# Tables of order, PSUM banks and engines replaced in a fused attention and mixer kernel

## The chip, the cores and the metric

The kernel runs on one core of a Trainium2 chip. A core has five engines that each work through their own list of instructions in order: TensorE (PE, matmuls; its weight loads are shown as PEld), VectorE (DVE), ScalarE (ACT), GpSimd (POOL), and SyncE (SP), which here only issues DMAs. Engines wait for each other on semaphores. Matmuls write to PSUM, a memory of eight banks of 512 fp32 columns on 128 partitions; everything else lies in SBUF. The metric is the device time of one run in microseconds (us), the median of several runs.

## The reference

Eight batches, eight heads, 576 positions, head size 64:

```
scores = (q @ k.T) / 8, block-causal mask of 64 x 64 blocks
attn   = softmax(scores) ; x = attn @ v, heads side by side -> x[576, 512]
theta  = x @ w_theta ; zr = x * cos(theta) ; zi = x * sin(theta)
y      = w_tok_r @ zr + w_tok_i @ zi        (mixing over positions)
u      = x + y
out    = u + relu(u @ w_ch)
```

All inputs are wide; weights arrive as 64-bit floats. The kernel splits most operands into a high and a low fp16 part and adds three products (high x high, low x high, high x low). Queries and keys of batches 0 to 2 are multiplied as fp32.

## The kernel before

**Parts.** The work is cut into 3,404 parts, each a Python function that emits one or a few instructions of one engine. `add(...)` enters a part with its key, what it needs, the PSUM labels that it takes, and the engines that may do it ("A" ACT, "D" DVE, "P" POOL). 371 labels take a PSUM bank, and 915 parts can run on more than one engine. Nothing else in the code decides the order: `emit` (L236) walks the table `ORDER` (L37), in which each number is a part, takes each label's bank from the string `BANKS` and each part's engine from the string `PLACES`. As engines work in order, `ORDER` fixes every engine's list, the DMA queue on SP included.

**Attention.** A pair is two heads of one batch; there are 32 pairs and 64 heads n. For pair p the parts are `s1` (wide scores, both heads, into the two-bank tiles s0 and s1, L589 and mask L596), `s2` (narrow scores, into two other banks), `sd` (first-row scores, L617, into 64 columns of bank 7). For head n: `m` (maxima, DVE, L633), `mn` (bias, L641), `e` (exponentials, ACT, L646), `high` and `low` (fp16 parts of the probabilities p, L431, L433, L436), `turn` (DMA transposition of p, L665), `weighted` (the sum with v, L680, into the output columns of bank 7), `normalise` (three DVE steps, L692, L694, L698), `half` (a small DMA). Heads of the first half of pieces (n < 16) come in two pieces, A and B; later ones as one, "all". The wide tiles exist once, so `s1` of a pair waits until the exponentials of the pair before have read them.

**Mixer.** For batch b: `xh`, `xl`, `xt` (parts of x and their transposition), `theta` (L816, L819), `turns`, `rest`, `size` and `sines` (angles, L828, L834, L849, L851), `z` (product with x, L860), `zh` and `zl` (its parts, L436), `mix` (L884), `xs` (L889), `u` (L893), `uh` and `ul` (L900), `c` (channel product, L907), `relu` (L913 or L915), `out` (L923), `store`. Every `theta`, `mix` and `c` group takes one of banks 0 to 6 until it is read.

**Weights.** At the start 17 blocks of weights (`w`) are loaded, narrowed and split on ACT, DVE and POOL, and their largest values found with matmuls (`wa`, L494).

**PSUM tiles.** The eight banks are six tiles: two tiles of two banks and four of one bank each. The framework orders accesses to a tile; bank 7 holds both the output sums and the first-row scores:

```python
two_banks = [ps.tile([P, 1024], F32, name=f"s{n}") for n in range(2)]
banks = [two_banks[n // 2][:, 512 * (n % 2):512 * (n % 2) + 512] for n in range(4)]
banks += [ps.tile([P, 512], F32, name=f"g{n}") for n in range(4, 8)]
o = o_bank[:, 0:NI * (D + 1)].rearrange("p (a c) -> p a c", a=NI)
s_first = [o_bank[:, 384 + 64 * i:448 + 64 * i] for i in range(2)]
```

Of the kernel before, what the change touches and what calls it, by code (L numbers as in the profile page):

```python
# [37 lines left out]
    8, 9, 158, 160, 335, 10, 11, 0, 1, 16, 17, 2, 56, 340, 364, 363, 372, 373, 374, 336, 339, 57, 40, 3, 350, 58,  # L38
    18, 24, 351, 32, 352, 59, 19, 41, 386, 42, 390, 375, 334, 341, 25, 26, 362, 20, 414, 353, 354, 48, 33, 376, 104,
    49, 164, 43, 338, 361, 365, 366, 34, 337, 355, 105, 342, 345, 391, 401, 162, 343, 27, 415, 35, 106, 107, 367,  # L40
    344, 50, 51, 72, 368, 369, 346, 165, 4, 385, 347, 402, 108, 403, 412, 64, 163, 166, 413, 65, 167, 404, 416, 66,
    73, 387, 417, 418, 5, 168, 28, 12, 169, 389, 13, 80, 392, 170, 67, 81, 82, 171, 21, 388, 172, 423, 383, 60, 74,
    83, 393, 161, 96, 97, 394, 98, 29, 136, 137, 395, 138, 139, 396, 159, 437, 36, 332, 99, 88, 75, 89, 90, 52, 466,
    100, 436, 424, 425, 441, 348, 442, 465, 91, 405, 333, 112, 349, 120, 397, 398, 464, 463, 439, 37, 44, 356, 357,
    438, 140, 84, 68, 22, 113, 121, 45, 53, 384, 358, 359, 452, 377, 114, 173, 76, 178, 370, 426, 176, 453, 61, 454,
    440, 427, 69, 77, 474, 443, 85, 475, 444, 447, 467, 378, 92, 419, 406, 399, 420, 93, 115, 101, 30, 141, 445,
    371, 122, 123, 142, 446, 151, 143, 144, 379, 14, 421, 180, 380, 116, 31, 434, 435, 468, 54, 381, 469, 70, 94,
    86, 448, 476, 487, 449, 489, 515, 491, 407, 128, 488, 455, 456, 494, 490, 6, 470, 471, 514, 518, 129, 495, 130,
    492, 493, 503, 519, 520, 504, 400, 408, 409, 410, 15, 145, 428, 360, 422, 516, 429, 505, 539, 131, 496, 430,
# [12 lines left out]
    155, 648, 649, 641, 95, 670, 646, 604, 611, 650, 693, 645, 1856, 669, 1868, 651, 1864, 1854, 656, 1855, 564,
    612, 1857, 652, 613, 698, 614, 615, 657, 658, 653, 654, 691, 694, 692, 720, 1858, 697, 678, 659, 633, 695, 626,
    1865, 1862, 699, 1859, 197, 634, 679, 680, 1866, 1867, 635, 696, 1908, 1909, 1863, 1910, 636, 1911, 689, 1889,
    660, 700, 701, 1914, 1870, 707, 681, 1915, 708, 709, 1872, 744, 1893, 119, 690, 1899, 1900, 719, 1885, 682, 702,
    637, 1871, 674, 703, 718, 1901, 1881, 655, 1916, 1876, 721, 661, 1917, 662, 1912, 710, 2004, 200, 722, 675, 723,
    2007, 724, 199, 683, 1888, 729, 704, 1894, 711, 1873, 1880, 730, 663, 1907, 676, 1892, 201, 664, 1918, 749,
    1895, 1896, 1913, 665, 1897, 725, 2005, 1919, 684, 1902, 1903, 1877, 677, 1898, 2008, 685, 731, 686, 687, 743,
    1884, 742, 1878, 1879, 1904, 202, 747, 748, 712, 1874, 705, 732, 733, 203, 713, 726, 1875, 785, 204, 195, 706,
    746, 745, 750, 1882, 1883, 205, 1886, 1887, 766, 765, 753, 1944, 1945, 1890, 206, 764, 755, 754, 767, 768, 2006,  # L70
    1938, 1946, 1939, 1891, 666, 156, 1940, 1941, 714, 715, 207, 1942, 716, 751, 752, 734, 1947, 790, 208, 756, 757,
    191, 826, 727, 728, 1948, 135, 1937, 740, 735, 741, 736, 1949, 771, 737, 738, 781, 772, 688, 1943, 769, 2009,
    717, 770, 773, 2010, 1905, 783, 787, 786, 1920, 784, 788, 789, 2023, 2011, 2024, 758, 807, 791, 759, 792, 796,
# [1103 lines left out]
```

## Time and profile before

| | |
|---|---|
| median of 3 runs | 668.34 us (667.21 to 670.35) |
| profiled execution, span | 668.2 us |
| PE busy | 615.9 us, 92% |
| DVE busy | 570.6 us, 85% |
| ACT busy | 508.4 us, 76% |
| POOL busy | 393.8 us, 59% |
| mean granted clock of PE | 0.959 |

The profile gives no other time of the profiled execution than its span, from the first to the last instruction. Busy time is the union of an engine's instructions; those of the same engine can overlap a little. Tiles are called by their names: "s" is a two-bank PSUM tile, "g" a one-bank PSUM tile, "t" the exponentials, "p" their parts, "pt" the transposed p, "xT" the transposed x (later the result). A granted clock of 1.00 is 2.4 GHz and 0.50 is 1.2 GHz.

### The profile page before, as it was taken

To read this page: it belongs to the slowest core of one execution; us is meant where nothing else is said; L and a number is where in the kernel's file an instruction comes from. 1 tells how busy PE (TensorE), PEld (TensorE's weight loads), DVE (VectorE), ACT (ScalarE), POOL (GpSimd) and SP (SyncE) were. 2 spreads that over 40 slices of the span, in tenths; PEclk is the share of its full clock that TensorE was granted. 3 is DMA by queue.
4 is the path that set the end of the run, shared out by engine and by line. 5 is a ranking of instruction groups with operands and counts; after the bars stand their busy time and mean duration, and the time that the engine had idled before them with its cause. 6 is when DMAs were issued, how large, how long until landed. Compare 5 with 4: busy or idle time off the path is not lost. (4 is left out here: it accounts for less than half of the span.)

```text
span 668.2 us, 18051 instructions
## 1 busy us (share of the span) xinstructions
PE 615.9 (92%) x7372; PEld 459.6 (69%) x7374; DVE 570.6 (85%) x1136; ACT 508.4 (76%) x776; POOL 393.8 (59%) x411
## 2 busy tenths in 40 slices
PE   5477796999999999999999998999999998999997
PEld 3155554876788578776778766875786586857775
DVE  4987897998998998989989889999998998846474
ACT  5997878776997998978998899889997986325111
POOL 4355564876575446564675748664777476673340
PEclk9578896999999999999999999999999998999999
DMA  8999999998989596989869897889797655840002
GB/s 347 381 235 231 207 165 196 248 197 147 233 197 214 126 242 122 194 170 183 220 169 169 164 222 164 192 169 202 186 207 156 120 89 117 172 82 1 19 36 88
DMA packets 268514, 116.57 MB, mean 174 GB/s; under 512 B 256016, under 2 KB 256016, under 8 KB 268432
## 3 DMA queue, kind: packets, MB, share of 16 engines
q1 hardware_dynamic: 268432, 115.43, 78.5%
q8 instruction: 57, 0.93, 0.6%
q14 instruction: 25, 0.20, 0.1%
HBM read 42.01 MB, written 9.44 MB: 77 GB/s over the span
## 5 line engine op out<-in xcount | busy, mean ns | idle before, releaser
L884 PEld LDWEIGHTS <-zh 128*128 128x128 f16 x1152 | 112.7, 98 | 30.4 <-issue 1.6
L884 PE MATMUL g<-wT_h,zh 128*128 128x288 f16 x405 | 115.9, 286 | 0.3 <-DVE xT L923 0.3
L884 PE MATMUL g<-wT_l,zh 128*128 128x288 f16 x405 | 115.8, 286 | 0.0
L884 PE MATMUL g<-wT_h,zl 128*128 128x288 f16 x405 | 115.8, 286 | 0.0
L680 PE MATMUL g<-v,pt 128*128 128x65 f16 x2880 | 104.8, 197 | 10.5 <-DVE xn L698 4.4
L680 PEld LDWEIGHTS <-pt 128*128 128x128 f16 x2880 | 101.0, 100 | 17.7 <-issue 9.6
L633 DVE TENSOR_REDUCE m<-s 128x1 f32<-128x576 f32 (+3 forms) x134 | 86.4, 668 | 12.0 <-PE s L596 11.8
L436 POOL TENSOR_TENSOR p<-t,p 128x512 f16<-128x512 f32 (+4 forms) x31 | 69.8, 2254 | 43.7 <-ACT p L431 26.5
L431 ACT CAST p<-t 128x1600 f16<-128x1600 f32 (+4 forms) x62 | 79.7, 1289 | 7.8 <-DMA pt<-p 6.8
L436 DVE TENSOR_TENSOR p<-t,p 128x1600 f16<-128x1600 f32 (+4 forms) x49 | 80.4, 1643 | 4.3 <-ACT p L431 3.8
L860 POOL TENSOR_TENSOR aa<-aa,xn 128x256 f32<-128x256 f32 (+1 forms) x63 | 51.5, 829 | 28.1 <-ACT aa L849 25.5
L816 PEld LDWEIGHTS <-xT 128*128 128x128 f16 x384 | 36.6, 98 | 43.8 <-DMA xT<-xp 2.4
L884 PEld LDWEIGHTS <-zl 128*128 128x128 f16 x576 | 56.4, 98 | 14.4 <-POOL m L641 0.4
L646 ACT ACTIVATE t<-s,m,size 128x576 f32<-128x576 f32 (+1 forms) x80 | 59.2, 777 | 8.1 <-POOL m L641 6.0
L907 PEld LDWEIGHTS <-wch_h 128*128 128x128 f16 x512 | 48.1, 98 | 14.7 <-issue 2.9
L633 DVE TENSOR_REDUCE m<-g 128x1 f32<-128x320 f32 (+2 forms) x154 | 53.5, 369 | 2.3 <-PE g L596 0.7
L646 ACT ACTIVATE t<-g,m,size 128x192 f32<-128x192 f32 (+2 forms) x100 | 49.2, 533 | 5.4 <-POOL m L641 3.5
L436 POOL TENSOR_TENSOR zl<-aa,zh 128x512 f16<-128x512 f32 (+1 forms) x38 | 44.7, 1181 | 12.9 <-PE g L617 6.9
L907 PE MATMUL g<-ul,wch_h 128*128 128x288 f16 x164 | 46.9, 286 | 2.8 <-DVE ul L900 2.8
L884 PE MATMUL s<-wT_l,zh 128*128 128x288 f16 x171 | 48.9, 286 | 0.0
L884 PE MATMUL s<-wT_h,zl 128*128 128x288 f16 x171 | 48.9, 286 | 0.0
L884 PE MATMUL s<-wT_h,zh 128*128 128x288 f16 x171 | 48.9, 286 | 0.0
(187 smaller groups left out, 1632.8 us busy)
## 6 DMA issues: line engine op xcount, KB each, us to landing
rv<-in_v SPq DMA_DIRECT2D x16, 768.0 KB, 5.3
rq<-in_q SPq DMA_DIRECT2D x16, 640.0 KB, 5.3
rk<-in_k SPq DMA_DIRECT2D x16, 576.0 KB, 5.5
out<-xT SPq DMA_DIRECT2D x32, 288.0 KB, 2.5
w_raw<-in_w_tok SPq DMA_DIRECT2D x5, 576.0 KB, 5.4
pt<-in_w_tok SPq DMA_DIRECT2D x4, 576.0 KB, 7.4
w_raw<-in_w_theta SPq DMA_DIRECT2D x4, 512.0 KB, 7.0
w_raw<-in_w_ch SPq DMA_DIRECT2D x4, 512.0 KB, 5.6
```

What stands on the lines that cost most here:

```text
L431: nc.scalar.copy(out=out, in_=x)
L436: engine_of(on).tensor_tensor(out=out, in0=x, in1=y, op=ALU.subtract)
L633: nc.vector.tensor_reduce(out=self.m[:, i:i + 1], in_=self.scores_of(i), axis=AX.X, op=ALU.max)
L646: nc.scalar.activation(out=t_parts[self.hh][:, to:to + n], in_=self.scores_of(i), func=AF.Exp, scale=self.scales()[0], bias=self.m[:, NI + ...
L680: nc.tensor.matmul(o[:, i, :], lhsT=source[:, block, :], rhs=vv[:, slot, hh, :], start=first, stop=last)
L816: nc.tensor.matmul(g, lhsT=xT[:, xx + i, :], rhs=ww[:, dt, :], start=first, stop=last)
L860: engine_of(on).tensor_tensor(out=cd, in0=cd, in1=self.xns[dt][:, i0:i0 + ni, :], op=ALU.mult)
L884: nc.tensor.matmul(g, lhsT=zz[:, kk, cols], rhs=ww[:, kk, ts], start=(n == 0 and kk == k0 and nn == 0), stop=n == 4 and kk == k0 + ni - 1 ...
L907: nc.tensor.matmul(g[:, 0:HS], lhsT=ww[:, dt, e * P:(e + 1) * P], rhs=uu[:, dt, th * HS:(th + 1) * HS], start=dt == 0 and n == 0, stop=dt ...
```

## The change

The three tables are replaced; no other line of the kernel changes, and the parts are the same. The diff, cut to the first lines of each table:

```diff
 ORDER = [
-    8, 9, 158, 160, 335, 10, 11, 0, 1, 16, 17, 2, 56, 340, 364, 363, 372, 373, 374, 336, 339, 57, 40, 3, 350, 58,
...
 BANKS = (
-    "4556164551001236001234501234601235601235401231001236501236401235401234601235601235601235601234501235401235401235"
...
+    "4504666153001236401236501234601234601235601235401231001234501236401235401234601235601235601235601234501235401235"
...
 PLACES = (
-    "DAAPDAPAAADAAAAAAPDAPDAAPAAAAAPAAPAAPAAPAADAAPADAAAAPDPPPPDDDDAPPDAPPAPDDDDAPPDADPPPDAPPPPADADPAPPAPPPPAPADPPDDP"
...
+    "DAPDAADAADAAPAAAAADAADAPPAADAADAADAADAAAAAAAAPAAPDADPADDPPPDPDPDAPADPDDPADDAPDPADDADPPPDADAPADPADPDDPPPPPADDAPPA"
```

With the numbers turned back into parts, PE's list begins as follows (the head of each list, to the end of the first theta; `s1.0` is the wide scores of pair 0):

```
before: s2.0 sd.0 s2.1 s1.0 s1.1 sd.1 wa.0 vm.0 wa.1-3 s2.2 s1.2 weighted.0.A wa.4 weighted.0.B sd.2 wa.5-10
        weighted.1.B wa.11 wa.12 weighted.1.A s1.3 sd.3 weighted.2.B s2.3 weighted.2.A weighted.3.A weighted.3.B s2.4
        weighted.4.A weighted.4.B s1.4 sd.4 weighted.5.A weighted.5.B sd.5 weighted.6.B wa.13-16 ...
after:  s2.0 sd.0 s1.0 sd.1 s2.1 wa.0 wa.1 s1.1 wa.2 wa.3 vm.0 wa.4 s2.2 s1.2 sd.2 wa.5 weighted.0.B weighted.0.A
        sd.3 wa.6-10 weighted.1.B wa.11 weighted.1.A wa.12 s1.3 s2.3 weighted.2.A weighted.2.B weighted.3.A sd.4
        weighted.3.B s2.4 sd.5 weighted.4.A weighted.4.B s1.4 weighted.5.A weighted.5.B wa.13-16 vm.1 weighted.6.B ...
```

71 of 371 bank entries and 327 of 915 engine entries differ. Engine entries before and after: POOL 367 and 331, ACT 295 and 296, DVE 253 and 288. By kind, on DVE before and after: `low` 49 and 58, `z` 61 and 73, `zl` 19 and 24, the third step of the weights 4 and 10, `qh` and `kh` 0 and 7, `v1` 2 and 4, `xh` 2 and 7, `relu` 28 and 24, `mn` 27 and 23, `size` 15 and 11, `xs` 15 and 13.

## Rows read from the trace of the kernel before

**Rows 1.** The page: busy us, share of span, instructions of each engine.

```profile
PE 615.9 (92%) x7372; PEld 459.6 (69%) x7374; DVE 570.6 (85%) x1136; ACT 508.4 (76%) x776; POOL 393.8 (59%) x411
```

**Rows 2.** Stretches: length, busy us by engine (instructions), clock, DMA share, GB/s.

```profile
0.00:20.00 20.00, 8.98 (x48) 6.18 (x48) 10.11 (x21) 10.56 (x18) 7.46 (x32) 0.99 0.92 353
20.00:40.30 20.30, 12.44 (x54) 7.00 (x57) 18.61 (x40) 19.69 (x36) 10.53 (x11) 0.50 0.98 322
40.30:84.60 44.30, 32.98 (x464) 26.12 (x463) 36.83 (x94) 36.57 (x65) 25.78 (x28) 0.81 1.12 223
84.60:134.00 49.40, 43.21 (x466) 30.29 (x465) 45.00 (x83) 39.46 (x63) 31.25 (x33) 0.86 0.98 205
134.00:550.00 416.00, 406.92 (x5267) 304.43 (x5264) 384.95 (x770) 363.04 (x537) 263.64 (x259) 1.00 0.85 178
550.00:668.20 118.20, 111.34 (x1093) 85.53 (x1089) 75.06 (x134) 39.09 (x63) 55.17 (x51) 0.99 0.33 75
```

**Rows 3.** PE in order of time, start: start us, length, instruction, [wait <-releaser].

```profile
10.45 2.19 PE L589 MATMUL g<-rk,rq 64*128 64x320 f32 x12
...
23.76 4.11 PE L589 MATMUL s<-rk,rq 64*128 64x512 f32 x16 [7.17 <-ACT t L646]
...
47.25 0.98 PE L680 MATMUL g<-v,pt 128*128 128x65 f16 x15 [2.14 <-ACT t L646]
...
73.52 0.43 PE L617 MATMUL g<-rk,rq 128*128 128x64 f32 x2 [1.11 <-DVE xn L698]
...
106.59 4.11 PE L589 MATMUL s<-rk,rq 64*128 64x512 f32 x16 [3.43 <-DMA rk<-in_k]
...
113.06 0.69 PE L617 MATMUL g<-rk,rq 128*128 128x64 f32 x2 [2.25 <-DVE xn L698]
```

**Rows 4.** Waits of PE from 134 us on: us in total, times, longest.

```profile
PE g L907 <- DVE ul L900: 2.8, 2, 2.6
PE s L907 <- ACT t L646: 2.5, 2, 1.9
...
PE g L680 <- DVE xn L698: 1.2, 2, 0.8
...
PE g L680 <- DVE m L633: 0.4, 1, 0.4
PE s L589 <- DVE xT L923: 0.3, 1, 0.3
PE g L589 <- ACT t L646: 0.3, 1, 0.3
PE g L884 <- DVE xT L923: 0.3, 1, 0.3
```

**Rows 5.** Waits of ACT over the whole span, two of them.

```profile
ACT s L913 <- PE s L884: 1.7, 1, 1.7
...
ACT t L646 <- DVE xn L698: 0.6, 1, 0.6
```

**Rows 6.** Groups by shape: count, busy us, mean ns of one, idle before.

```profile
L900 DVE SCALAR_TENSOR_TENSOR ul<-u,u_scales,uh 128x576 f16<-128x576 f32 x32 | 29.8, 940 | 2.4 <-POOL uh L427 1.5 <-ACT uh L423 0.6
...
L436 DVE TENSOR_TENSOR p<-t,p 128x1536 f16<-128x1536 f32 x15 | 26.6, 1773 | 0.5 <-issue 0.3 <-ACT p L431 0.2
L860 DVE TENSOR_TENSOR rr<-rr,xn 128x256 f32<-128x256 f32 x28 | 14.8, 529 | 0.0
...
L436 DVE TENSOR_TENSOR zl<-rr,zh 128x512 f16<-128x512 f32 x9 | 7.4, 820 | 0.0
...
L436 DVE TENSOR_TENSOR p<-t,p 128x512 f16<-128x512 f32 x3 | 2.3, 769 | 0.0
```

**Rows 7.** In order of time, 550 to 555 us.

```profile
550.42 3.41 POOL L436 TENSOR_TENSOR p<-t,p 128x1600 f16<-128x1600 f32 x1
550.79 3.66 DVE L900 SCALAR_TENSOR_TENSOR ul<-u,u_scales,uh 128x576 f16<-128x576 f32 x1
...
554.50 0.28 PE L907 MATMUL g<-ul,wch_h 128*128 128x288 f16 x1 [2.58 <-DVE ul L900]
```

More of the change, by code (lines that the diff above doesn't have):

```diff
@@ L37 @@
 ORDER = [
[176 rows of a table removed]
[171 rows of a table added]
 ]
 BANKS = (
-    "4556164551001236001234501234601235601235401231001236501236401235401234601235601235601235601234501235401235401235"
-    "4012346012354012346012346012345012354012356012356012346012356012365012346012364012365012365246551650445606454041"
-    "6540151630666461566050425316646355451406665420444500465601466501605440544155446405425450164156455646416040451634"
-    "52245163452601620132435450513216524"
+    "4504666153001236401236501234601234601235401231001234501236401235401234601235601235601235601234501235401235401235"
@@ L220 @@
+    "4012346012354012346012346012345012354012356012356012346012356012365012346012364012365012365246511650445606454021"
+    "6540151344666061566050435256666455450616566350154500465601415661602510544155446450425420154166455546416040451626"
+    "34532653264501205145632130623406543"
 )
 PLACES = (
-    "DAAPDAPAAADAAAAAAPDAPDAAPAAAAAPAAPAAPAAPAADAAPADAAAAPDPPPPDDDDAPPDAPPAPDDDDAPPDADPPPDAPPPPADADPAPPAPPPPAPADPPDDP"
-    "DDPPPDAPPAPPADPPDDPADPAPPADPAPADADPADDADPAPAPADDADPPAPPPDPPADPADAPADPADAADPADDAPAAPPADPAPAAADADPADPPADADPADAPADA"
@@ L229 @@
-    "DAAADAPPAPPPAPDPAPPDAPPPPPPDPPPPAPPPPPPDPPDDAPDADAPDDADDAAAADAAPPDAPPDDDDADPDAPDPADDDAPDPPDDPADPPDDDDAPDPPPPPDPP"
-    "PADDADDPDPPDDADAAAA"
+    "DAPDAADAADAAPAAAAADAADAPPAADAADAADAADAAAAAAAAPAAPDADPADDPPPDPDPDAPADPDDPADDAPDPADDADPPPDADAPADPADPDDPPPPPADDAPPA"
+    "DPAPADAPPDPPADPPDDPADPADPADPADAPADPADPADPAPAPADPADAPAPPPDPPADPADAPADPDDDAADADDAPAAAPADPAPAAAPADPADDPDDADPADAPADA"
+    "DPADADAPDDPAPAAAPADPADPPPPADPAPDDPDAPDADAAAPPPDADAAPDADPADDPAPADPADAAADADPADAAAPADDPDDPPDADDAPAPAPADDADAAAPADPAP"
@@ new lines @@
+    "AAADDDPAPAAPDAPPDPPPPPADDADPPPPPDAPADAAAPPPDPDAPPPPDDDADPPAPDDAPPPAPDPAPPDAPPPPDPADDPDDDAADADADAADADAPDDDAAAADDP"
+    "PDDPPPPAPPPAPPDAPPDAPPDADDDAPPPPPDDPDPADADAPPDAADAAAAAPAPAPDDAAADDPPAPDPPDDPAPPDPDPPDPDDAPPDAPPPAPPDADDPAPPPPAPP"
+    "PDADAAAAAAAPPPDPDDADAADPPADPPAPDPAPDPPDDDAPPPAPDDAPPDPDDDAPPDAPPAPAPAPPDDAADDDDADAPAPADDAAAAPPAPPDPPPPPPPPPPDDAP"
+    "DDAPDDAPPDAPDPAPDPDPDADAPAPADDAADAADADDPAPAPAADAAPPPDPPPPDPPPDPADPPPDPDAPDDADPDAPDDAPPDDPDAPPPDDAAAAADDAADPADAPD"
+    "DAAADAPPPDPDAPPDPPDDPDPDAPDPAPPPADPPADDPAPPPAPDDPDDDPAADDAADAAADPPPPADDAAADPDADPDPPDDPPPDPPDPPPDPADDPPPPDDDPDADD"
@@ L231 @@
+    "PPPDPDPDAPADDAAAADA"
 )
```

5 lines of the change are left out of this document (removed), and 346 rows, old and new, of the table ORDER.

## The prediction, made before the result was known

> **What bounds the kernel now.** I read the busy shares first. TensorE (PE) is busy 615.9 of 668.2 us [rows 1], so the time is PE's work plus PE's idle time plus what the half-speed clock costs. The stretches say where the idle time lies. Subtracting PE busy from the length of each stretch [rows 2] gives 11.0, 7.9, 11.3 and 6.2 us of idle in the four stretches up to 134 us (36.4 us together), 9.1 us in the 416 us from 134 to 550, and 6.9 us after that. So PE is 98% busy from 134 us on, and 73% before. The granted clock is 0.50, 0.81 and 0.86 of full speed from 20 to 134 us: its lower level, 1.2 GHz, is granted in stretches where PE has been idle, and it is 1.00 where PE is always fed.
>
> The other engines show who makes PE wait. VectorE (DVE) is busy 385.0 of 416 us from 134 to 550 (92.5%), ScalarE (ACT) 87%, GpSimd (POOL) 63% [rows 2]. So in the long middle PE is the bound, and DVE is the next one, 31 us of idle away from it. Up to 134 us no engine is full: between 20 and 134 us DVE is busy 100.4 of 114 us and ACT 95.7, and PE stands still for chains that run through both. The largest single waits of PE there are 7.17 us for an exponential of ACT, 3.43 us for the load of k, 2.25 and 1.11 us of the first-row scores for the normalisation's read of the output bank, and 2.14 us of a weighted sum for an exponential [rows 3]. After 134 us the waits are a dozen small ones, 2.8 us for DVE's low part of u and 2.5 us for exponentials the largest [rows 4].
>
> **The change part by part.** *What stays.* The 3,404 parts and their arithmetic are the same, so PE has the same 7,372 matmuls. Only gaps, clock and waits can move. Laid side by side, the tables are near twins: adding up the matmul time of PE's new list, the PE work ahead of each pair's wide scores differs from the old by at most 2 us for the pairs I compared.
>
> *Order at the start.* The old list has PE run the narrow scores of pair 1 before the wide scores of pair 0; the new one has them after (s2.1 behind s1.0). Those 12 matmuls take 2.19 us and stand just ahead of the wide scores [rows 3]. The wide scores of pair 1 later wait 7.17 us for pair 0's last wide exponential. With pair 0's scores ready 2.2 us sooner, and ACT's new list with some 2.6 us less weight conversion ahead of that exponential (11.6 us instead of 14.2 by the shortest record of each kind), I take 2.2 us off this wait. It carries to the end only if what is late next moves too: DVE, with 5 to 6 us more ahead of the last maxima of pairs 2 and 3.
>
> *First-row scores and the output bank.* Bank 7 holds the output sums and the 64 columns of first-row scores. sd.4 stood behind its pair's wide scores and waited 1.11 us for the previous head's normalisation; now it lies between the two pieces of one head's sum, where no read stands before it, so 1.1 us go. weighted.1.B waited 2.14 us for the exponential of first-row scores of pair 2; pair 2's first-row scores are now issued ahead of weighted.0.B instead of behind weighted.0: about half of that wait goes, 1.1 us. sd.6, with 2.25 us, stays where it was [rows 3]. Of these 4.4 us (2.2, 1.1, 1.1) I count half, 2.2 us: DVE and ACT are at 88% and 84% there, so half of a freed gap fills with their next lateness. Bounds: 4.4 us gained, or nothing.
>
> *Waits inside a PSUM tile in the middle.* Banks 0 and 1 are one tile, 2 and 3 another. A rectification waited 1.7 us for a mixing matmul, which never writes its bank; and an exponential 0.6 us for a normalisation, though both only read [rows 5]. So accesses to one tile do wait on each other, and a list made without them has PE arrive too early. Of PE's waits after 134 us I put 5.0 us to that class: 2.5 us for exponentials (a channel product in a wide-score bank), 1.2 and 0.4 us of the weighted sum, 0.3 us three times for exponentials or bank releases [rows 4]. 71 of 371 bank entries change. Counting places in the lists where PE comes back to bank 7 after a read with under 1.5 us of PE work between, there are 12 before and 9 after; the two-bank tiles have 8 before and 6 after. That is a modest thinning (and weighted.50 now follows weighted.49 with nothing between): I take half, 2.5 us. Bounds: 5.0 us, or a loss of 2 us if new tight places weigh more.
>
> *Engines.* POOL loses 36 entries, DVE gains 35, ACT gains one. The three largest kinds on DVE: nine low parts p (at most six of 0.77 and three of 1.77 us, 9.9 us), twelve z products (0.53, 6.4 us) and five low parts of z (0.82, 4.1 us) [rows 6], 20.4 us. DVE casts of q and k are not in the trace; seven of them between 0.53 and 0.82 us [rows 6] are 4 to 6 us. The rest nearly cancels against fewer rectifications, biases and absolute values. I take 22 us on DVE: about 7 before 134 us, 13 from 134 to 550, the rest behind. What hides them is DVE's idle: 31 us of 416 shrink to 18, 95.7% busy. If that cover fails wholly, 13 us come out on PE; if DVE was never the late one, 0. The nearest row is the only big stall DVE made, 2.58 us [rows 7], and its cause is not DVE's load: I take 0.8 us.
>
> That row shows something else. The low part of u that PE waited for took 3.66 us on DVE, against 0.94 us on average [rows 6, 7]. It began 0.37 us into a POOL low part of 3.41 us and ended 0.62 us behind it. The Trainium skill, SBUF — State Buffer (Who interferes with whom), says that a DVE instruction with two SBUF inputs contends with a GpSimd one that reads SBUF, and that the later of the two blocks fully. By that rule this trace agrees, and each low part taken off POOL would free DVE as well as POOL. The sum would then have no charge for DVE, 663.5 us.
>
> **Sum.** The profiled execution took 668.2 us, 0.1 below the median of the three runs, 668.34. 668.2 - 2.2 - 2.5 + 0.8 = 664.3 us.
>
> **Rivals.** *A, the forecast:* 664.3, from 661 to 667. *B, the gains are displaced:* every gap removed turns into another, since lists of equal length with equal PE work ahead of each pair leave the same chains. For it: sd.6, the wait for k at 106.6 us and the chain through the sines stay where they were. Against it: the first order change is real. 668 us. *C, slower, DVE becomes the bound between 134 and 550 us:* DVE's work there rises to 398 us. If it must stand idle for as long as before, 31 us, the stretch takes 429 us, 13 us more: 681; if for 24.5 us, 422.5, 6.5 us more: 674.7 us, which I take. It decides from where DVE still needs more than 18 us of its idle. For it: 95.7% leaves little room, and a list in fixed order can't use a gap that comes at the wrong place. Against it: POOL's share falls with it, so that DVE's inputs come sooner. *D, POOL's unloading frees DVE, and all of the start's gaps close:* 4.4 us at the start, 5.0 us in the middle and 2.6 us of the stall at 554.5 [rows 7]; 668.2 - 12.0 = 656.2. Against it: the POOL low part that blocked DVE at 550.4 is still POOL's in the new table, and still next to that ul. *That the change does not count what it says* would look like B.
>
> **How the numbers follow.** A 0.50, B 0.22, C 0.16, D 0.12. A measurement of this kernel tells about 0.5% from no change, that is 665.0 and 671.7 us. Of A's range the part below 665.0 holds 0.62; with D and a little of B faster is 0.31 + 0.12 + 0.03 = 0.46. No change: 0.18 of A, 0.17 of B, 0.03 of C, 0.38. Slower: 0.16. The range reaches from D to most of C: 656.5 to 673.5 us. The likeliest case alone has 661 to 667.
>
> **What would show it.** The wait of the second wide scores under 5.5 us (7.17 before); sd.4 without a wait for the normalisation; PE idle before 134 us near 34 us; PE waits on exponentials and normalisation after 134 us near half of 5.0 us; DVE near 592 us busy, POOL near 355. Wrong: DVE over 96% between 134 and 550 with PE idle above 12 us there (C); the clock staying low longer at the start, or PE idle unchanged in both parts (B).

## The result: slower by 1%

| | before | after |
|---|---|---|
| median, 4 runs each | 668.19 us (667.21 to 670.35) | 674.45 us (673.61 to 675.86) |
| ratio | | 1.0098 (95%: 1.007 to 1.0125) |
| span of the profiled execution | 668.2 us | 674.0 us |

The changed kernel is 6.3 us slower. The time was forecast at 664.3 us, with a gain as the likeliest outcome; the direction was wrong. Wherever a run's time and span are both on record, the time is 1.7 to 2.2 us longer. So the profiled execution of the old kernel, with a span of 668.2 us, is most likely the slowest of its four, 670.35 us. In the profile after, a line of the kernel has a number smaller by 6 (by 5 in the kernels of the experiments).

The page's busy times, as in [rows 1]:

```profile
PE 614.9 (91%) x7374; PEld 452.8 (67%) x7374; DVE 589.5 (87%) x1171; ACT 507.1 (75%) x777; POOL 351.1 (52%) x375
```

VectorE has 18.9 us more, GpSimd 42.7 us less: 592 and 355 had been forecast. The stretches, with the columns of [rows 2]:

```profile
0.00:20.00 20.00, 9.10 (x52) 5.88 (x52) 11.06 (x25) 11.21 (x19) 6.48 (x33) 1.00 0.93 365
20.00:40.30 20.30, 11.99 (x56) 6.70 (x56) 19.67 (x41) 20.27 (x37) 5.92 (x7) 0.62 1.14 317
40.30:84.60 44.30, 33.23 (x473) 26.28 (x474) 38.97 (x94) 35.09 (x61) 19.76 (x25) 0.79 1.03 230
84.60:134.00 49.40, 42.22 (x482) 29.20 (x481) 45.78 (x97) 42.59 (x69) 29.44 (x36) 0.97 1.00 205
134.00:550.00 416.00, 398.79 (x5133) 293.21 (x5133) 388.06 (x765) 353.62 (x525) 226.28 (x222) 1.00 0.82 174
550.00:674.00 124.00, 119.57 (x1185) 91.49 (x1180) 85.92 (x153) 44.35 (x71) 63.24 (x57) 1.00 0.38 81
```

From 134 to 550 us TensorE stands idle for 17.2 us (416 less 398.79), where it was 9.1. VectorE is busy for 93.3% of it, hardly more than before; by this row alone it is not the bound. But the row cuts at the same times, not at the same work; the section on VectorE's load below has the cut at equal work. At the start TensorE, in order of time, answers to [rows 3]:

```profile
10.54 4.11 PE L583 MATMUL s<-rk,rq 64*128 64x512 f32 x16
...
20.80 3.59 PE L583 MATMUL s<-rk,rq 64*128 64x512 f32 x16 [4.00 <-ACT t L640]
...
29.89 0.26 PE L368 MATMUL g<-diag,ones 128*128 128x128 bf16 x1 [4.31 <-POOL diag L362]
...
56.44 0.77 PE L674 MATMUL g<-v,pt 128*128 128x65 f16 x11 [2.93 <-DVE xn L692]
...
107.59 0.43 PE L611 MATMUL g<-rk,rq 128*128 128x64 f32 x2 [2.54 <-DVE xn L692]
```

The first two rows are the wide scores of pairs 0 and 1: the second waits 4.00 us, not 7.17. New waits stand behind it (4.31, 2.93). TensorE's waits behind 134 us, as in [rows 4]:

```profile
PE g L674 <- DMA pt<-p: 2.8, 4, 1.2
PE g L674 <- DVE xn L692: 2.7, 4, 1.2
PE g L901 <- DVE u L887: 2.4, 1, 2.4
PE g L901 <- DVE ul L894: 1.6, 1, 1.6
PE s L901 <- ACT t L640: 1.3, 2, 0.9
PE s L810 <- ACT t L640: 1.3, 1, 1.3
PE g L583 <- DVE xT L917: 1.2, 2, 0.6
PE s L368 <- POOL diag L362: 1.0, 1, 1.0
```

Those on exponentials are hardly less (1.3 and 1.3; 2.5 and 0.3 before), and those on the normalisation `xn` have grown (2.7; 1.2 before), as have those on `xT` (1.4 in all; 0.8 before) and on the transposed probabilities `pt` (2.8; 1.1 before, not among the lines of [rows 4]). The wait for VectorE's `u` is new. The 2.58 us at 554.5 us [rows 7] are gone, but its like stands at 328 us: a low part on GpSimd, `ul` right behind it, and a TensorE that waits.

```profile
327.75 3.15 POOL L430 TENSOR_TENSOR p<-t,p 128x1536 f16<-128x1536 f32 x1 [3.62 <-ACT p L425]
...
327.86 3.66 DVE L894 SCALAR_TENSOR_TENSOR ul<-u,u_scales,uh 128x576 f16<-128x576 f32 x1
...
331.57 0.28 PE L901 MATMUL g<-ul,wch_h 128*128 128x288 f16 x1 [1.62 <-DVE ul L894]
```

**Where the time goes.** Since all kernels here have the same matmuls, I added up the columns that TensorE streams in each trace (an fp32 column four times, a half array half) and compared when equal work was reached. The table gives how far a kernel's profiled execution is behind (+) the old kernel with one letter changed (run `e6` below, which follows the old tables to 545 us). Rows are by the time at which that one reached the work.

| e6 at | before | after | e3 | e7 | e8 | e9 | e12 | e13 | e16 |
|---|---|---|---|---|---|---|---|---|---|
| 146.8 us | 3.2 | -1.4 | -1.4 | -2.7 | -3.4 | -2.7 | 2.0 | -3.0 | -0.9 |
| 287.6 us | 3.3 | 2.4 | -1.2 | -1.2 | 0.3 | 0.4 | 3.5 | 0.9 | 2.3 |
| 351.9 us | 3.4 | 8.7 | -0.4 | -0.5 | 2.8 | 6.6 | 8.7 | 6.1 | 8.7 |
| 484.0 us | 3.5 | 11.8 | -0.2 | 0.2 | 2.8 | 7.5 | 15.2 | 9.2 | 17.1 |
| 656.8 us | 5.4 | 10.8 | -0.3 | -0.5 | 2.9 | 8.9 | 16.6 | 7.9 | 16.0 |

The column "before" is a caution: the same lists ran 3.3 us later in the first 130 us of that one execution. Of the 4.6 us by which "after" leads "before" at 147 us, most is that; what the new start is worth has to come from many runs.

### The profile page after: what moved, and what is told of

Same layout as the page of the kernel before. It is cut to its first block, busy times and chain, and to the rows that moved or that the text cites. A ratio compares the mean times of both kernels' runs of the same rounds, so it can differ in the third digit from the quotient of the medians.

```text
span 674.0 us, 18045 instructions
## 1 busy us (share of the span) xinstructions
PE 614.9 (91%) x7374; PEld 452.8 (67%) x7374; DVE 589.5 (87%) x1171; ACT 507.1 (75%) x777; POOL 351.1 (52%) x375
## 4 chain that ended last, share of the span: by engine, by line
PE 37%; DVE 10%; ACT 10%; issue 4%; DMA 4%; POOL 3%; SPq 0%; DVEq 0%; POOLq 0%; ACTq 0%
PE g L878 11%; PE s L878 5%; PE s L810 4%; ACT t L640 4%; PE g L674 4%; PE g L901 3%; DMA pt<-p 3%; PE g L810 3%; PE s L901 3%; ACT p L425 2%; DVE m L627 2%; DVE p L430 2%; PE s L583 2%; PE g L583 1%; ACT aa L843 1%
## 5 line engine op out<-in xcount | busy, mean ns | idle before, releaser
L674 PE MATMUL g<-v,pt 128*128 128x65 f16 x2880 | 102.4, 196 | 13.2 <-DMA pt<-p 7.3
L674 PEld LDWEIGHTS <-pt 128*128 128x128 f16 x2880 | 98.3, 99 | 20.1 <-DMA pt<-p 9.7
L430 DVE TENSOR_TENSOR p<-t,p 128x1600 f16<-128x1600 f32 (+4 forms) x58 | 89.6, 1547 | 7.5 <-ACT p L425 7.4
L627 DVE TENSOR_REDUCE m<-s 128x1 f32<-128x576 f32 (+2 forms) x132 | 85.0, 673 | 4.5 <-PE s L590 4.3
L425 ACT CAST p<-t 128x1536 f16<-128x1536 f32 (+4 forms) x64 | 81.2, 1276 | 3.9 <-issue 2.1
L430 POOL TENSOR_TENSOR p<-t,p 128x1536 f16<-128x1536 f32 (+4 forms) x22 | 57.5, 2615 | 51.1 <-ACT p L425 38.9
L854 POOL TENSOR_TENSOR aa<-aa,xn 128x256 f32<-128x256 f32 (+1 forms) x56 | 41.8, 755 | 45.8 <-ACT aa L843 39.1
L640 ACT ACTIVATE t<-g,m,size 128x320 f32<-128x320 f32 (+2 forms) x100 | 50.0, 534 | 12.6 <-DVE m L635 6.1
L627 DVE TENSOR_REDUCE m<-g 128x1 f32<-128x192 f32 (+2 forms) x156 | 54.4, 372 | 2.4 <-PE g L590 1.0
L901 PE MATMUL g<-uh,wch_h 128*128 128x288 f16 x160 | 45.9, 287 | 2.6 <-DVE u L887 2.4
```

The lines of the kernel that those rows point to most:

```text
L425: nc.scalar.copy(out=out, in_=x)
L430: engine_of(on).tensor_tensor(out=out, in0=x, in1=y, op=ALU.subtract)
L627: nc.vector.tensor_reduce(out=self.m[:, i:i + 1], in_=self.scores_of(i), axis=AX.X, op=ALU.max)
L640: nc.scalar.activation(out=t_parts[self.hh][:, to:to + n], in_=self.scores_of(i), func=AF.Exp, scale=self.scales()[0], bias=self.m[:, NI + ...
L674: nc.tensor.matmul(o[:, i, :], lhsT=source[:, block, :], rhs=vv[:, slot, hh, :], start=first, stop=last)
L854: engine_of(on).tensor_tensor(out=cd, in0=cd, in1=self.xns[dt][:, i0:i0 + ni, :], op=ALU.mult)
```

## The experiments

Each ratio, with its 95% interval, is to the old kernel run beside it (medians 666.1 to 668.1 us). Gains and losses in us are worked out from the ratio; the two medians alone can give up to 1.6 us more or less (for e3 1.3 us of gain instead of 2.8). Tables are told as parts: "P" is GpSimd, "D" VectorE, "A" ScalarE.

### Which table, and which stretch

**e1**, **e2**: the engine letters of one table with the order and banks of the other, behind about 150 us.

```diff
 e1: ORDER, BANKS new
-    PLACES new
+    PLACES new for the first 784 parts, old behind
 e2: ORDER, BANKS old
-    PLACES old
+    PLACES old for the first 784 parts, new behind
```

> The new order and banks throughout; the new engine table for the first 784 parts of the order (to about 150 us), the old one for all later parts (252 entries differ there, DVE doing a net 31 fewer). Theory 1 (load): the new kernel lost 10 us after 150 us because its engine table gives DVE about 13 us more work there; then most of the loss goes and the start's 4.5 us stay: 664 to 668 us. Theory 2 (order): the loss sits in the new order itself, at places where an engine meets another at the wrong moment, whatever the engines; then 672 us or more.

> The complement: the old order and banks throughout, the old engine table for its first 784 parts, the new one for all later parts. Theory 1 (load): DVE gets the added work and the time rises by the loss of 8 to 10 us, 676 to 678 us. Theory 2 (order): the old order keeps its places, 667 to 670 us. If both this and the other mixture are slow, the two tables only fit each other and neither theory alone holds.

Measured: e1 711.5 us, ratio 1.0664 (1.0623 to 1.0705); e2 747.15 us, 1.1203 (1.1145 to 1.1262). Letters and order fit only each other: either half alone costs far more than both. So neither "the new letters" nor "the new order" can be blamed by swapping a whole table, and this pair tells nothing of the 6 us.

**e3**, **e4**: all three tables changed over at one place.

```diff
 e3: first 784 parts (to about 150 us): new ORDER, BANKS, PLACES
-    the rest new
+    the rest old
 e4: first 868 parts old
-    the rest old
+    the rest new
```

> The new tables (order, banks, engines) for their first 784 parts, the old tables for all the rest. PE was 4.5 us ahead of the old kernel at equal work there. If the start's gain is real and carries through the old middle: 663 to 665 us. Rival (displaced): the old middle's chains eat it, 667 to 669 us.

> The old tables for their first 868 parts, the new tables for all the rest. If the loss of 10 us belongs to the new tables after 150 us, it comes out without the start's gain: 676 to 679 us. If the loss was only the start's gain running into a fixed limit (PE or DVE could not have used it), the time is about that of the new kernel or less, 668 to 674 us.

Measured: e3 664.85 us, 0.9958 (0.9936 to 0.9981), 2.8 us (1.3 to 4.3) faster than the old kernel; e4 680.76 us, 1.0227 (1.0167 to 1.0287). The new start is a gain, and it carries to the end; the loss belongs to the new tables behind 150 us. From 0.9958 to 1.0098 these cost 9.3 us. (e4 also loses 6 us at its join, near 180 us.)

**e7**: new start, old middle, new end.

```diff
 first 784 parts new
-parts to the 2796th (about 515 us) new
+parts to the 2796th old
 the rest new
```

> New tables for the first 784 parts (to about 150 us), old tables to the 2796th part (about 515 us), new tables for the rest. The new kernel regained 3.5 us on the old one near 555 us, where the old one stalls for 2.58 us, and the mixture with old tables to the end has that stall too. Theory 1 (the new tables are worse only in the middle): 1 to 4 us below the mixture that keeps the old tables to the end, ratio to the old kernel 0.990 to 0.995. Theory 2 (what the new end regains is only a part of what its own middle lost, since old and new lists there have the same work): the same as that mixture, ratio 0.9945 to 0.998, or above 1 if the join itself costs.

Measured: 662.58 us, 0.9949 (0.9924 to 0.9975). It is the fastest version here and beats both kernels; that it beats e3 too (0.9958) lies inside the intervals.

**e8**, **e9**: new tables up to 310 and up to 350 us, old ones behind.

```diff
 e8: first 1596 parts new
-    the rest new
+    the rest old
 e9: first 1910 parts new
-    the rest new
+    the rest old
```

> New tables for the first 1596 parts (to about 310 us), old tables for the rest. Between 146 and 250 us the changed kernel lost the 4.5 us that it had gained at the start, and from 311 us on it lost 8 more. Theory 1 (each loss is local to its stretch of the tables): the time is near the old kernel's, ratio 0.998 to 1.003, without the waits of 2.41 and 1.62 us at 324 and 332 us. Theory 2 (the lateness is stored in VectorE's and ScalarE's lists by what the new tables put on them before 310 us, and comes out whichever tables follow): ratio 1.005 to 1.01.

> New tables for the first 1910 parts (to about 350 us), old ones after. New tables to 310 us and old ones after came to 1.0013 of the old kernel. In the trace of the changed kernel TensorE falls 4 to 5.7 us back between 311 and 350 us, whatever single item is taken out there. Theory P (that loss belongs to the tables of these 40 us): ratio 1.006 to 1.010 and a lag that stays level behind 350 us. Theory H (the loss there is lateness that earlier tables stored up, or comes back later under the old tables): ratio 0.999 to 1.004.

Measured: e8 667.46 us, 1.0013 (0.999 to 1.0037); e9 673.88 us, 1.0081 (1.0056 to 1.0107). Some 4.5 us (0.0068; by the two intervals 2.1 to 6.9 us) come from the tables of 40 us. Reckoned as in the table above, the lag of e9 grows from 0.9 us at 310 us to 6.6 at 352, and then to 7.5 at 484. e8 loses 1.8 us near its own change of tables.

**e20**: the complement of it.

```diff
 new throughout
-parts 1640 to 1970 (about 318 to 360 us) new
+parts 1640 to 1970 old (34 letters)
```

> The complement: the changed kernel with the old tables in the parts 1640 to 1970 alone (about 318 to 360 us, 34 engine letters differ from the changed kernel's), new ones before and behind. Theory P: the waits of 2.41 and 1.62 us at 324 and 332 us go, and the kernel is 3 to 5.5 us below the changed one, ratio 1.002 to 1.006. Theory H, or a join that costs what it saves: ratio 1.008 to 1.014.

Measured: 673.06 us, 1.0072 (1.0047 to 1.0097), between the two expectations. The waits for `u` and `ul` are 0 and 0.52 us, but 3.11 us for `xT` stand at 332.67. Old lists may not meet here what the new ones left ahead of them, but no run shows it. The profiled execution, the slowest of its six (675.94 us), was also granted a mean clock of only 0.88 from 309.9 to 339.4 us. Inconclusive.

### Single late items

**e5**, **e11**, **e13** change single parts of the new tables around 311 to 333 us.

```diff
 e5:
-    low.35 P
+    low.35 D
 e11:
-    ... z.3.0.0.1 P, z.3.1.4.0 P, qh.19 P ... z.3.1.3.1 D
+    ... qh.19 P, z.3.0.0.1 P, z.3.1.4.0 P ... z.3.1.3.1 P
 e13: both
```

> The changed kernel with one letter of its engine table changed: the low part low.35 is worked by VectorE instead of GpSimd. In the trace of the changed kernel the low part of u for token rows 2, feature piece 3 (ul.2.3) took 3.7 us on VectorE, beginning 0.2 us behind the start of low.35 on GpSimd (3.2 us); TensorE then waited 1.62 us for it, and it lay 4.5 us further behind the old kernel after these 27 us than before. Theory 1, the collision of two SBUF reads costs what TensorE waited: ul.2.3 goes back to 0.8 us, the 1.62 us wait goes, low.35 costs VectorE 1.8 us; 674.45 becomes 672 to 673.5. Theory 2, the time lost there is the lateness of the whole VectorE list (mn.34 handed to GpSimd, e.34 later), of which the collision is only the visible end: ul.2.3 is 0.8 us but another wait stands in its place, 674 to 676.

> The changed kernel with two small edits ahead of its longest wait in the middle (2.41 us at 323.65 us, the channel product c.2.0.1.0 for VectorE's u.2.3.0): the high part qh.19 stands ahead of the rotary products z.3.0.0.1 and z.3.1.4.0 on GpSimd (it stood behind them, and z.3.1.4.0 waits for the last sine until 318.8 us, so that VectorE's ql.19 began only at 320.2 after 1.1 us of idle), and z.3.1.3.1 (0.8 us ahead of u.2.3.0 on VectorE) is GpSimd's again, as in the old tables. Theory 1 (single late items in a fixed order make the loss): u.2.3.0 comes 1.5 to 2 us sooner, the wait falls under 1 us, and the kernel is 1.5 to 3 us below the changed one (ratio to the old 1.005 to 1.008). Theory 2 (VectorE's load as a whole is what is late, so that any item taken out is replaced by the next): the loss of some 4 us between 311 and 338 us stays, ratio 1.009 to 1.0115.

> Both edits of the run before (qh.19 first, z.3.1.3.1 on GpSimd), and low.35 on VectorE, so that neither the late u.2.3.0 nor the slow ul.2.3 is there. Theory 1: the waits of 2.41 and 1.62 us both go, and the kernel is 2 to 4 us below the changed one (ratio 1.003 to 1.007). Theory 2: as without low.35 moved, or worse by its 1.8 us on VectorE; ratio 1.008 to 1.012.

Measured: 673.6 us, 1.0109 (1.006 to 1.0157); 673.75 us, 1.0104 (1.0079 to 1.0129); 674.01 us, 1.0124 (1.0085 to 1.0163). None gave anything back that can be told from the changed kernel's 1.0098, though each edit did what it should. In e5 `ul` is itself again, with the low part now VectorE's, right behind it:

```profile
325.91 0.80 DVE L895 SCALAR_TENSOR_TENSOR ul<-u,u_scales,uh 128x576 f16<-128x576 f32 x1
326.64 1.75 DVE L431 TENSOR_TENSOR p<-t,p 128x1536 f16<-128x1536 f32 x1
```

In e11 the wait for `u` falls from 2.41 to 0.61 us, and that for `ul` grows to 2.54:

```profile
318.71 0.30 PE L902 MATMUL g<-uh,wch_h 128*128 128x288 f16 x1 [0.61 <-DVE u L888]
...
327.55 0.40 PE L902 MATMUL g<-ul,wch_h 128*128 128x288 f16 x1 [2.54 <-DVE ul L895]
```

In e13 both are short, and the next thing that VectorE makes, `xT`, is late by 2.27:

```profile
320.30 0.30 PE L902 MATMUL g<-uh,wch_h 128*128 128x288 f16 x1 [0.61 <-DVE u L888]
...
327.29 0.28 PE L902 MATMUL g<-ul,wch_h 128*128 128x288 f16 x1 [0.70 <-DVE ul L895]
...
331.07 0.72 PE L584 MATMUL g<-kh,qh 64*128 64x320 f16 x2 [2.27 <-DVE xT L918]
```

In e11 and e13 the wait moves to the next part of one engine, whichever part is mended. This is what an engine without room would show. A stretch of equal TensorE work bears that out. Columns as in [rows 2]; the third busy time is VectorE's. The old kernel:

```profile
311.50:334.10 22.60, 21.93 (x336) 17.61 (x333) 22.15 (x49) 22.21 (x33) 14.71 (x15) 1.00 0.89 235
```

e8, whose lists are old again here; then the changed kernel; e13; and e5:

```profile
310.90:333.60 22.70, 22.00 (x341) 17.55 (x338) 21.93 (x48) 22.26 (x33) 14.57 (x15) 1.00 0.72 205
```

```profile
311.10:338.10 27.00, 22.23 (x340) 17.05 (x338) 25.72 (x49) 22.56 (x33) 13.23 (x16) 1.00 0.83 220
```

```profile
309.50:335.50 26.00, 22.28 (x340) 17.07 (x339) 25.45 (x49) 22.62 (x33) 13.13 (x16) 1.00 0.86 229
```

```profile
308.20:335.00 26.80, 23.69 (x340) 18.35 (x338) 25.52 (x50) 22.60 (x33) 10.53 (x15) 0.94 0.84 221
```

In the old kernel TensorE (97%), VectorE (98%) and ScalarE (98%) are all full in these 22.6 us. The new lists put 3.6 us more of VectorE's time here (25.72 less 22.15), and the stretch is 4.4 us longer: the 3.6, and most of 1.0 us in which VectorE waits for `qh.19`. The 3.6 us are `ul` at 3.66 us (2.9 more than 0.8), a second `ql` that came over from an earlier place (0.9), and a `kl` of 1.27 instead of 0.88, less what left. e13 has no such wait and no slow `ul`, but low.35's 1.75 us on VectorE instead: 25.45 us busy, 26.0 long. e9, with the new lists up to 350 us, is like the changed kernel (25.61 us of 26.9).

e5 is not so plain. Its 1.62 us wait is gone and no other stands in its place, but TensorE, which stood idle for 2.4 us for `u` just before, was granted a mean clock of 0.94, and its busy time is 23.69 us instead of 22.23. e11 has the same (0.94; 23.62). So up to 1.5 us that these two edits might have given may have gone into the clock. e13, at 1.00, lost nothing that way.

### VectorE's load by itself

**e12**: the load that the prediction had priced at 0.8 us, put on the old kernel alone.

```diff
 old ORDER, BANKS
-low.25, low.27, low.32, low.35, low.37, low.40, low.49  P
+low.25, low.27, low.32, low.35, low.37, low.40, low.49  D
```

> The old kernel with seven low parts of the exponentials between 250 and 480 us (heads 25, 27, 32, 35, 37, 40, 49) on VectorE instead of GpSimd: 7 times 1.77 = 12.4 us more on VectorE there, which is the load that the change was predicted to add between 134 and 550 us, with order and banks left alone. Theory 1 (only what stands at a tight place costs): each is worth 0 to 1 us, ratio 0.998 to 1.006. Theory 2 (the bound is VectorE's load in that stretch: with less than 24.5 us of idle it sets the time): VectorE needs 397 + 24.5 = 422 us for the stretch, 6.5 us more, ratio 1.008 to 1.012.

Measured: 678.01 us, 1.0172 (1.0127 to 1.0216): 11.5 us for 12.4 us of work, more than the load theory had asked for. VectorE's busy time is 584.0 us, 13.4 more. In the 22.6 us of above it has 1.6 us more, and the stretch is 1.6 us longer. So far this is an engine without room:

```profile
313.00:337.20 24.20, 22.28 (x337) 17.68 (x338) 23.76 (x49) 21.85 (x33) 14.86 (x18) 1.00 0.85 222
```

The next stretch is not. First the old kernel, then e12:

```profile
334.10:355.30 21.20, 21.08 (x268) 16.67 (x266) 18.33 (x39) 18.99 (x28) 15.27 (x18) 1.00 0.74 171
```

```profile
337.20:360.60 23.40, 21.20 (x268) 16.70 (x266) 19.97 (x42) 18.80 (x29) 12.14 (x13) 1.00 0.62 142
```

Here VectorE was busy for only 86% in the old kernel, with 2.87 us idle. 1.6 us more work made the stretch 2.2 us longer, and VectorE's idle time did not shrink (3.43 us). One wait for ScalarE grew from 0.3 to 2.8 us. The middle as a whole is alike. This is the TensorE work that the old kernel does from 134 to 550 us, in the changed kernel and in e12:

```profile
129.80:558.60 428.80, 411.59 (x5249) 303.37 (x5247) 400.06 (x793) 364.19 (x543) 237.08 (x230) 1.00 0.82 173
```

```profile
132.80:561.00 428.20, 410.08 (x5260) 305.64 (x5258) 397.65 (x776) 361.78 (x537) 249.76 (x251) 1.00 0.83 173
```

The old kernel needs 416.0 us for it, with 31.0 us of VectorE idle [rows 2]. In e12 VectorE has 12.7 us more work, the stretch is 12.2 us longer, and the idle time is still 30.6 us. In the changed kernel it is 15.1 us more work, 12.8 us longer, and 28.7 us idle. So the idle time hid almost nothing, and mostly not because VectorE was full: it waited for other engines as long as before. The largest of these waits in the old kernel are 6.4 us for ScalarE's `aa` and 3.5 us for TensorE's scores; in e12 they are 6.1 and 4.4. That these engines were late because VectorE had been late for them fits, but no run shows it by itself. It is no fixed price either: e8 has 8.8 us more VectorE work over the same TensorE work, is 3.8 us longer, and its idle time falls to 26.1 us. (e12's profiled execution also had the lower clock twice, near 384 and 568 us, at up to 1.7 us each; the changed kernel's had it nowhere from 134 to 670 us.)

**e15**, **e16**: load taken off VectorE, new order kept. **e17**: the same in the old kernel.

```diff
 e15: new tables
-    low.32, low.37, low.49  D
+    low.32, low.37, low.49  P
 e16: and eleven of zl, xl between 150 and 515 us
-    D
+    P
 e17: old tables
-    low.31, low.38, low.44, low.50  D
+    low.31, low.38, low.44, low.50  P
```

> The changed kernel with the three low parts that it took from GpSimd in the middle (heads 32, 37, 49) given back: 3 times 1.77 = 5.3 us less on VectorE, order and banks and all other letters new. Theory 2 (VectorE's load in the middle is what the time follows; 12.4 us more on it cost the old kernel 11.2 us): 4 to 5 us below the changed kernel, ratio to the old 1.002 to 1.005. Theory 1 (the loss sits in order and single places; the low parts are late on GpSimd at 3.3 us each): no gain or a loss, ratio 1.009 to 1.015.

> As the run before, and eleven low parts of z and of the token features (zl, xl; 0.82 us each on VectorE) given back to GpSimd as well: 5.3 + 9.0 = 14.3 us less on VectorE between 150 and 515 us. Theory 2: the loss of the middle goes, 8 to 10 us below the changed kernel, ratio 0.995 to 0.999. Theory 1: between the changed kernel and worse, since GpSimd's low parts come late for the matmuls that need them; ratio 1.006 to 1.02.

> The old kernel with four low parts in the middle (heads 31, 38, 44, 50, where GpSimd stood idle for 4 us behind the high part) on GpSimd instead of VectorE: 7.1 us less on VectorE. Theory 2, if it holds in both directions: 4 to 6.5 us faster, ratio 0.990 to 0.994. Rival: the slope holds upward only (VectorE's load bounds once it is raised; in the old kernel TensorE is 98% busy there and has no more than 9 us to give), or VectorE is slowed beside GpSimd as at 550 us: ratio 0.997 to 1.005.

Measured: e15 677.42 us, 1.014 (1.0104 to 1.0177); e16 678.58 us, 1.0169 (1.0136 to 1.0201); e17 670.2 us, 1.0034 (1.0003 to 1.0064). None is faster than the kernel that it starts from. e16 and e17 are slower; e15's interval overlaps the changed kernel's. The load theory fails in this direction. (Of e16's loss up to 3.4 us may be clock: its profiled execution had the lower level twice, near 324 and 467 us.) The profile shows that the load did not go. VectorE's busy time in e16 is 592.1 us, against 589.5 in the changed kernel, though 13.5 us of parts had left (5.2 of `p`, 8.3 of low parts of z and of the token features). Groups of VectorE in the changed kernel (busy us, mean ns):

```profile
L430 DVE TENSOR_TENSOR p<-t,p 128x1600 f16<-128x1600 f32 (+4 forms) x58 | 89.6, 1547 | 7.5 <-ACT p L425 7.4
...
L854 DVE TENSOR_TENSOR aa<-aa,xn 128x256 f32<-128x256 f32 (+1 forms) x40 | 20.2, 508 | 2.3 <-ACT aa L843 1.2 <-ACT aa L845 1.1
L560 DVE SCALAR_TENSOR_TENSOR kl<-rk,size,kh 128x576 f16<-128x576 f32 x20 | 18.0, 901 | 0.1
L555 DVE SCALAR_TENSOR_TENSOR ql<-rq,size,qh 128x640 f16<-128x640 f32 x20 | 17.6, 879 | 1.0 <-POOL qh L421 1.0
...
L635 DVE TENSOR_SCALAR m<-m,size 128x5 f32<-128x5 f32 (+1 forms) x16 | 5.1, 316 | 0.3
```

and in e16:

```profile
L431 DVE TENSOR_TENSOR p<-t,p 128x1600 f16<-128x1600 f32 (+4 forms) x55 | 84.4, 1535 | 9.5 <-ACT p L426 9.4
...
L855 DVE TENSOR_TENSOR aa<-aa,xn 128x256 f32<-128x256 f32 (+1 forms) x40 | 22.5, 566 | 2.3 <-ACT aa L844 1.2 <-ACT aa L846 1.1
L561 DVE SCALAR_TENSOR_TENSOR kl<-rk,size,kh 128x576 f16<-128x576 f32 x20 | 21.4, 1070 | 0.1
L556 DVE SCALAR_TENSOR_TENSOR ql<-rq,size,qh 128x640 f16<-128x640 f32 x20 | 19.2, 959 | 1.1 <-POOL qh L422 1.1
...
L636 DVE TENSOR_SCALAR m<-m,size 128x5 f32<-128x5 f32 (+1 forms) x16 | 8.6, 536 | 0.4
```

Three low parts are gone (5.2 us), and the same number of `aa`, `kl`, `ql` and `m` take 10.8 us more. In e17 likewise: `ul` 33.3 us for the 29.8 of [rows 6], 5.0 us of low parts gone (four of 1.77 us would be 7.1), busy 574.4 us against 570.6. What is handed to GpSimd comes back as VectorE's waiting for it, inside its own instructions. Single rows of e16 show it, with two of the low parts handed back, each beside one VectorE instruction:

```profile
302.28 3.50 POOL L431 TENSOR_TENSOR p<-t,p 128x1600 f16<-128x1600 f32 x1 [5.95 <-ACT p L426]
...
302.63 3.77 DVE L561 SCALAR_TENSOR_TENSOR kl<-rk,size,kh 128x576 f16<-128x576 f32 x1
...
462.55 3.70 POOL L431 TENSOR_TENSOR p<-t,p 128x1536 f16<-128x1536 f32 x1
...
463.22 3.06 DVE L636 TENSOR_SCALAR m<-m,size 128x4 f32<-128x4 f32 x1
```

`kl` begins 0.35 us into the low part and ends 0.62 us behind it; `m` begins 0.67 us into one and ends 0.03 us behind it. The Trainium skill, SBUF — State Buffer (Who interferes with whom), has the later one of a VectorE instruction with two SBUF inputs and a reading GpSimd one wait for the whole of the other; `kl`, `ql`, `ul` and `aa` have two tensor inputs, and for them the trace agrees. The bias `m`, with one, is not covered by that sentence and waited as well. The way back is not symmetrical: in e12 GpSimd lost seven low parts and VectorE's time rose by all of them, since `ul` became 2.9 us shorter but `aa` 3.4 us longer.

**e6**: the stall of [rows 7].

```diff
 old tables
-low.60 P
+low.60 D
```

> The old kernel with one letter of its engine table changed: low.60 on VectorE instead of GpSimd. In the old kernel's trace ul.5.2 took 3.66 us on VectorE beginning 0.37 us into low.60, and TensorE waited 2.58 us. Theory 1 (the collision alone makes the stall): ul.5.2 near 0.9 us, the wait of 2.58 us goes or falls under 0.8 us, and the kernel is 1 to 3 us below the old one (ratio 0.9955 to 0.9985). Theory 2 (the stall is displaced: VectorE takes the 1.8 us of low.60 in the same place, so that the next waits grow by as much): ratio 0.9985 to 1.002.

Measured: 664.71 us, 0.9972 (0.9948 to 0.9996), 1.9 us. But the wait has only changed its name:

```profile
553.26 0.31 PE L584 MATMUL g<-kh,qh 64*128 64x320 f16 x2 [2.21 <-DVE xT L918]
```

What the trace of the old kernel has more is a spell of half clock behind the stall, at a cost of 1.7 us (below, on the hardware). e3 has the stall and no half clock, and from 484 us on it takes as long as e6 (-0.2 and -0.3 us in the table). So by these traces the edit itself gave next to nothing; how much of the 1.9 us it is stays open.

### The start

**e14**: the prediction's step alone. **e18**: the new letters alone.

```diff
 e14: old tables
-    s2.1, w.5.2, m.2.1, high.1.B, s1.0
+    s1.0, s2.1, w.5.2, m.2.1, high.1.B
 e18: old ORDER, BANKS
-    PLACES old
+    PLACES new for the first 784 parts, old behind
```

> The old kernel with one part moved: the wide scores of pair 0 stand ahead of the narrow scores of pair 1, not behind them, as the prediction's step for the start has it; all else is old. Theory 1 (that order alone gives what the new tables gain at the start): the wait of 7.17 us of the second wide scores falls to 5 us, and 1.5 to 2.8 us carry to the end, ratio 0.9955 to 0.998. Theory 2 (VectorE's and ScalarE's new lists at the start are needed too): the wait moves to other places and less than 1 us carries, ratio 0.9985 to 1.002.

> Old order and banks throughout; the engine letters are the new ones for the first 784 parts (76 letters differ) and the old ones after. New order, banks and letters together gave 2.8 us there, and the order of pair 0's wide scores alone lost 3.5. Theory A (the letters carry the start's gain, ScalarE's shorter conversion list above all): 1.5 to 3 us faster, ratio 0.9955 to 0.998. Theory B (letters and order only fit each other): slower, ratio 1.002 to 1.01.

Measured: e14 669.82 us, 1.0052 (1.003 to 1.0074); e18 681.98 us, 1.0215 (1.0177 to 1.0252). This step of the new order is slower alone, and so are the new letters alone; with the rest of the new order they are together 2.8 us faster (e3). The new order with the old letters was not run. In e14 the wide scores of pair 0 now wait for an exponential themselves, and pair 1's for longer than the 7.17 us of [rows 3]:

```profile
12.12 4.11 PE L584 MATMUL s<-rk,rq 64*128 64x512 f32 x16 [1.60 <-ACT t L641]
...
25.51 3.15 PE L584 MATMUL s<-rk,rq 64*128 64x512 f32 x10 [7.68 <-ACT t L641]
```

## Why the prediction was wrong

*What bounds the kernel.* This reading failed first: "in the long middle PE is the bound, and DVE is the next one, 31 us of idle away from it." The 92.5% are a mean over 416 us. From 311.5 to 334.1 us VectorE was at 98% already, and that stretch alone gave 4 to 5 of the 9.3 us that the new middle cost. The Trainium skill, Perfetto Trace Analysis (Optimization Strategy), says that the most-contended engine may change over a kernel's time; the trace agrees, down to stretches of 20 us (TensorE is at 98% over the 416 us, but in this stretch at 97%, with VectorE and ScalarE at 98%). Elsewhere the 31 us were VectorE's waiting, which stayed. Three readings were slips that change no term. TensorE is busy for 97% from 134 us on, not 98 (518.3 of 534.2 us). The largest waits ahead of that left out 7.6 us for the first load, and waits of 2.3 and 2.0 us. And the span of 668.2 us was set beside the median time, 668.34, as if both were times.

*The start, -2.2 us.* The size was right: -2.8 us (-4.3 to -1.3) by e3, and the wait for the second wide scores is 4.00 us, under the 5.5 that were asked for. The reason is not shown. The prediction took the order of the wide scores and ScalarE's shorter list together; that order alone lost 3.5 us (e14) and the new letters alone 14 (e18). sd.4 lost its wait and weighted.1.B its 2.14 us, as forecast, but the piece of a sum right ahead of sd.4 now waits 2.93 us for a normalisation; sd.6 waits 2.54 instead of 2.25 us. The gain seems to be one of order and letters together, and part of what looked like a gain in the traces was one late execution of the old kernel. TensorE's idle time before 134 us did not fall to 34 us; it is 37.5.

*Waits inside a PSUM tile, -2.5 us.* Not seen. The waits of the kinds that had been counted at 5.0 us, half of it to go, are 7.9 us behind 134 us: 2.6 on exponentials, 2.9 on `xn`, 1.0 on `m`, 1.4 on `xT`. Counting tight places in the lists was no price, probably because whether a place is tight depends on when VectorE reaches it. That the class of waits cost nothing was not tested alone.

*VectorE's load, +0.8 us.* This is the step of the sum that failed: "What hides them is DVE's idle". The work was counted rightly (22 us; 18.9 by busy time), but e12 prices 12.4 us of it in the middle at 11.5 us, not 0.8. The wrong choice was the value between 0 and 13 us: the only big stall that VectorE made was taken as the nearest row. VectorE's busy time in short stretches would have been nearer for the stretch at 98%, but not for the next one, at 86%, which lost as much. What failed is the step itself: over equal TensorE work the idle time that was to be the cover stayed, 28.7 us in the changed kernel and 30.6 in e12, of 31.0.

*The skill's rule, with 663.5 us.* The collision is real (`ul` 3.66 us behind a low part, 0.80 without), but "each low part taken off POOL would free DVE as well" is wrong as a sum, and with it the 663.5 us: VectorE's time rose by all that it was given in e12, and did not fall by what it gave up in e15 to e17.

*Rivals.* C came to 674.7 us, nearly the measured time, and that is luck. The runs support its first form, "it must stand idle for as long as before", with 429 us for the middle: at equal work it is 428.8 us, with VectorE busy for 400.1 where 398 had been said. C's 681 us came from that; the start, 4.2 us earlier in the profiled executions, and the end, 2.8 us shorter, bring the span down. C chose the smaller loss of 6.5 us instead, with nothing for start and end. Its sign, over 96% busy, could not come: an idle time that stays leaves the share at 93.3%. D is refuted by its own step (freeing). B would have left 668. The stall at 554.5 us is gone in the changed kernel, as D's sum had it, and the total rose all the same.

*Still open:* 2 to 4 us lost between 150 and 290 us and 3 between 352 and 484 (table above, "after" and e13 against e3). Waits of 0.86 us at 180 and 1.17 at 483 for `xn`, and 1.03 at 408 for `m`, stand there, all VectorE's; none was taken out by a run. That VectorE's added work makes the whole 9.3 us is argued from e12 and the equal cut, not shown: where it was taken out of the changed kernel (e15, e16), VectorE's busy time did not fall.

## What to carry to other kernels

Do not call an engine's idle time a cover for added work before seeing what it waits for there: with lists in a fixed order, 12.7 us more on VectorE left its idle time at 30.6 of 31.0 us. Compare kernels at equal work of the engine that bounds, in stretches of some 20 us; by the clock the same engine's share seems not to move. Where several engines are full together (98% in one stretch, in a mean of 92%), mending one late instruction can just make the next one late. Moving work between VectorE and GpSimd isn't a transfer of its duration: look at what the other's instructions then take. And tables that were found together can't be judged by halves; cut both over at one time instead.

## What the runs showed of the hardware

The granted clock did not fall behind every pause of the same kind. Behind the stall of 2.58 us the profiled execution of the old kernel was granted 0.66 over 5 us, that is the lower level for a part of it:

```profile
555.00:560.00 5.00, 5.00 (x64) 3.11 (x62) 3.30 (x9) 2.04 (x3) 0.63 (x1) 0.66 0.27 54
```

In e3 the same stall, for the same `ul` (2.58 us at 550.5), left it at full speed:

```profile
551.00:556.00 5.00, 4.78 (x101) 3.57 (x99) 4.42 (x13) 2.67 (x4) 1.07 (x3) 1.00 0.26 50
```

The same stall for `ul`, of 2.57 to 2.59 us, is in three more profiled executions: the 5 us behind it were granted 0.67 in e9, 0.66 in e14 and 1.00 in e17. In e8, where the stall is one of 2.89 us for `xT`, it was 0.66. Why it falls in some and not in others stays open here.

Two executions of the same lists (before and e6) differed by 3.2 us at 147 us and then kept this distance within about 0.4 us for 380 us; at the half clock behind the stall they part by 1.9 us more. The first 130 us, with their DMA waits and half clock, are where these two scatter.

Small VectorE instructions can wait for GpSimd's as well as large ones: a 128x4 bias took 3.06 us in e16 beside a low part, and the 16 biases 536 ns on average instead of 316.
